# The last output projection of a decode kernel: two column strips, B's sum ahead of it, and five weight loads

## The chip, the cores and the metric

The kernel runs on one core of a Trainium2 chip (trn2). The time is what the device takes for one execution, in microseconds (us); executions of one kernel are repeated and the median is quoted. A profiled execution also gives a trace: what each engine did, when each DMA landed, and which share of its full clock TensorE was granted. "Span" is the time from the first to the last instruction in the trace; it is about 2 us shorter than the time.

PE is TensorE's matmul side, PEld its weight loads, DVE is VectorE, ACT ScalarE, SP SyncE (here the engine that issues the DMAs; SPq is its queue).

## The reference, cut to what matters

Two attention blocks decode one token each. Block A has 32 heads with 32768 keys; block B has 8 key/value heads for 32 query heads, with the last 4096 keys. Each ends in an output projection of a vector of 4096 values with a 4096x512 matrix, and the two results of 512 values are concatenated:

```python
def _A_ref(x, k_cache, v_cache, wq, wo):
    ...
    p = _softmax(scores, axis=-1)
    o = jnp.einsum("bhqk,bhkd->bhqd", p, v_cache)
    return (lambda x, *d: x.transpose(*d))(o, 0, 2, 1, 3).reshape(B, Sq, H * Dh) @ wo
# _B_ref: the same over the last W = 4096 keys, each key/value head used by four query heads
a = _A_ref(A_x, A_k_cache, A_v_cache, A_wq, A_wo)
b = _B_ref(B_x, B_k_cache, B_v_cache, B_wq, B_wo)
return jnp.concatenate([a, b], axis=-1)          # shape (1, 1, 1024), bf16
```

Caches and weights are bf16; what the kernel reads of them is 570 MB.

## The kernel before

The kernel streams K and V of A's 32 heads through on-chip buffers (8 MB each of K and V a head, back to back on SP's queue) and works on each head while the next arrives. B is done at the start, except for its output projection. After the last V the queue brings the two output matrices: B's in two loads, A's in four. Each output matrix lies as 128 partitions by 32 "rows" of 512 columns, so a projection is 32 matmuls that add up, each with one column of the attention vector as the 128x1 stationary operand and 512 weight columns as the moving operand. (This text calls one of those 32 steps a row.)

B's 32 rows run in four column strips of the array at once (output partitions 0, 32, 64, 96), whose four partial sums must be added at the end by one more matmul, with a column of ones and zeros (the trace shows it as two). A's 32 rows run one after the other, full width, into output partition 0.

```python
WO_CUTS = {"A": (0, 12, 22, 28, 32), "B": (0, 16, 32)}     # rows per load

def proj_part(self, name, part, out):
    a0, a1 = self.WO_CUTS[name][part:part + 2]
    ...
        for a in range(a0, a1):
            row, pos, begin, end = out(a)
            inst = e.matmul(row, lhsT=oz[:, a:a + 1], rhs=wo[:, 512 * a:512 * a + 512], start=begin, stop=end,
                            tile_position=pos, skip_group_check=True)
    return self.op("pe", mm, (self.wosem[name][part], 16), self.c[name]["ozop"])   # waits for that load

def store(self, name, bank, off, dep):
    o = self.op("dve", lambda v: v.tensor_copy(self.out_sb[0:1, off:off + 512], bank[0:1, :]), dep)
    self.op("sp", lambda e: e.dma_start(self.out[0, :, off:off + 512], self.out_sb[0:1, off:off + 512]) ..., o)

def emit_proj(self):
    for part in range(len(self.WO_CUTS["B"]) - 1):           # B: four strips
        o = self.proj_part("B", part, lambda a: (self.S[32 * (a % 4):32 * (a % 4) + 1, :], (0, 32 * (a % 4)), a < 4, a >= 28))
    strips = self.op("dve", lambda v: v.tensor_copy(self.pb[:, :], self.S[:, :]), o)
    for part in range(len(self.WO_CUTS["A"]) - 1):           # A: one full-width row after the other
        last = self.proj_part("A", part, lambda a: (self.PT[0:1, :], None, a == 0, a == 31))
        if part == 0:                                        # the sum of B's strips, after A's first part
            o = self.op("pe", lambda e: e.matmul(self.ACC[0:1, :], lhsT=self.e32[:, 0:1], rhs=self.pb[:, :], ...), strips, self.accread)
            self.store("B", self.ACC, 512, o)
    self.store("A", self.PT, 0, last)
```

## Time and profile before

| | before |
|---|---|
| median time, us | 1331.5 (six executions, 1329.72 to 1331.80) |
| span of the profiled execution (a seventh, 1331.99 us), us | 1329.9 |
| PE busy / DVE busy | 73% / 57% |
| DMA | busy almost throughout, 429 GB/s on average |
| A's last weights landed, us from the start | 1324.1 |
| A's last matmul done | 1327.6 |

The page's first two parts for the kernel before: the busy time of the engines, and the busy tenths of the DMA engines in 40 equal slices of the span.

```profile
PE 970.0 (73%) x13402; PEld 682.1 (51%) x13402; DVE 751.7 (57%) x1345; ACT 54.8 (4%) x167; POOL 2.3 (0%) x17
...
DMA  9999999999999999999999999999999999999997
```

The stream of bytes bounds the kernel: DMA is at 9 tenths or more in every slice but the last. Only in that last slice is there anything to gain in the projection, so all other views are of the last 14 us.

The DMA issues of the kernel before, over the end of the run: source and destination, count, size, and us from issue to landing.

```profile
kbuf<-in_A_wo_dram SPq DMA_DIRECT2D x1, 1536.0 KB, 28.1
kbuf<-in_A_wo_dram SPq DMA_DIRECT2D x1, 1280.0 KB, 30.8
kbuf<-in_A_wo_dram SPq DMA_DIRECT2D x1, 768.0 KB, 32.1
kbuf<-in_A_wo_dram SPq DMA_DIRECT2D x1, 512.0 KB, 32.9
```

They are issued at 1289.88, 1290.25, 1290.72 and 1291.21 us and land at 1317.93, 1321.03, 1322.85 and 1324.09.

The chain of waits that ended last, in order of time (start, length, what), of the kernel before:

```profile
1289.88 28.05 DMA kbuf<-in_A_wo_dram
1317.93 0.04 issue
1317.98 4.41 PE psPT L649 x12
1322.39 0.89 PE psACC L667 x2
1323.27 4.33 PE psPT L649 x20
1327.60 0.02 issue
1327.63 0.68 DVE out_sb L655
```

From the first landing on, PE never waits again: 12 rows, the sum of B's strips, 20 rows. It is 3.5 us (1327.60 - 1324.09) behind the last landing. Twelve rows took 4.41 us, but the last twenty 4.33 us; the windows say why. They give for each stretch its length, the busy time of PE, PEld, DVE, ACT and POOL (with counts), then the granted clock, the DMA share and GB/s.

```profile
1318.00:1321.00 3.00, 3.00 (x10) 1.01 (x11) 0.00 (x0) 0.00 (x0) 0.00 (x0) 0.65 0.91 370
1321.00:1322.00 1.00, 1.00 (x4) 0.28 (x3) 0.00 (x0) 0.00 (x0) 0.00 (x0) 0.50 0.45 186
1322.00:1323.00 1.00, 1.00 (x3) 0.21 (x2) 0.00 (x0) 0.00 (x0) 0.00 (x0) 0.84 0.25 100
```

PE got half its clock for about 3.4 us, from 1318.9 to 1322.3. A row of 512 columns takes 0.427 us there and 0.216 us at full clock, while a row's weights arrive every 0.31 us (20 rows in 6.1 us). So PE keeps up with the loads at full clock, and falls behind at half.

The end of the kernel before, from the timeline (start, length, engine, line, operation, tiles, count, and the idle time before it with what ended it):

```profile
1327.63 0.68 DVE L655 CAST out_sb<-psPT 1x512 bf16<-1x512 f32 x1 [3.64 <-PE psPT L649]
1328.33 0.25 SPq L656 DMA_DIRECT2D out_dram<-out_sb  x1
```

The store is issued at 1328.33 and, by the trace's completion records, lands at 1329.43, 1.10 us later.

### The profile page before, as it was taken

The page shows a single profiled execution, that of the slowest core. Times are in us where ns is not written, and L with a number is a line of the kernel's source. Part 1 is how long each engine was busy: PE and PEld are TensorE (multiplying, and loading weights), DVE is VectorE, ACT ScalarE, POOL GpSimd, SP SyncE. Part 2 cuts the span into 40 slices and gives each one's busy share as a digit, 9 for nine tenths or more (in the row PEclk, how much of TensorE's full clock was granted, in tenths as well). Part 3 has the DMA queues.
Part 4 walks back from the last instruction along what each step waited for, and adds up shares of the span by engine and source line. Part 5 has one row for each costly group of instructions (what it writes and reads, how often), then busy time and mean ns, then how long its engine had stood idle before and what let it go on. Part 6 is the DMA issues. An engine that isn't in the chain of part 4 may idle for free.

```text
span 1329.9 us, 28729 instructions
## 1 busy us (share of the span) xinstructions
PE 970.0 (73%) x13402; PEld 682.1 (51%) x13402; DVE 751.7 (57%) x1345; ACT 54.8 (4%) x167; POOL 2.3 (0%) x17
## 2 busy tenths in 40 slices
PE   3756678687677878767787876778777776877786
PEld 3544456554445655444465544446554444655552
DVE  3654466655556666554566655456665545666562
ACT  0000000000000000000000000000000000000000
POOL 0000000000000000000000000000000000000000
PEclk9767898878879887887988788798878779888888
DMA  9999999999999999999999999999999999999997
GB/s 391 432 432 435 437 428 432 436 438 430 432 434 434 436 432 434 430 440 432 434 430 440 432 432 430 442 430 434 430 440 432 432 432 440 432 432 432 433 435 306
DMA packets 12931, 570.66 MB, mean 429 GB/s; under 512 B 1522, under 2 KB 1524, under 8 KB 1780
## 3 DMA queue, kind: packets, MB, share of 16 engines
q1 hardware_dynamic: 12628, 570.43, 99.3%
q8 instruction: 12, 0.20, 0.1%
q10 hardware_dynamic: 288, 0.00, 0.0%
q14 instruction: 3, 0.02, 0.0%
HBM read 570.43 MB, written 0.00 MB: 429 GB/s over the span
## 4 chain that ended last, share of the span: by engine, by line
DMA 69%; PE 28%; DVE 2%; issue 0%; ACT 0%; SPq 0%
DMA kbuf<-in_A_k_cache_dram 64%; PE psT L491 24%; PE psS L513 4%; DMA kbuf<-in_B_k_cache_dram 3%; DMA kbuf<-in_A_wo_dram 2%; DVE kt L494 1%; PE psPT L649 1%; PE psACC L593 0%; SPq L286 0%; DVE oc_A L609 0%; PE psACC L667 0%; PE psPT L565 0%; ACT psb L541 0%; DVE tr_in L530 0%; DVE out_sb L655 0%
## 5 line engine op out<-in xcount | busy, mean ns | idle before, releaser
L494 DVE COPY kt<-psT 128x1024 bf16<-128x1024 bf16 x1056 | 656.5, 685 | 245.4 <-PE psT L491 243.8
L491 PE MATMUL psT<-ident,kbuf 128*128 128x128 bf16 x8448 | 582.9, 235 | 174.1 <-DMA kbuf<-in_A_k_cache_dram 162.1
L491 PEld LDWEIGHTS psT<-ident,kbuf 128*128 128x128 bf16 x8448 | 543.5, 107 | 266.5 <-DMA kbuf<-in_A_k_cache_dram 170.2
L593 PE MATMUL psACC<-vbuf,ptsb 128*4 128x512 bf16 (+1 forms) x2112 | 181.0, 517 | 22.8 <-ACT ptsb L568 22.0
L513 PE MATMUL psS<-kt,qw 128*32 128x512 bf16 x2048 | 157.6, 385 | 15.5 <-DVE kt L494 15.5
L607 DVE TENSOR_SCALAR oc_A<-psACC,hot_A 128x128 f32<-128x128 f32 x32 | 11.2, 351 | 245.0 <-PE psG L620 245.0
L593 PEld LDWEIGHTS psACC<-vbuf,ptsb 128*4 128x4 bf16 (+1 forms) x2112 | 58.6, 109 | 135.3 <-issue 84.9
L541 ACT ACTIVATE psb<-psS,nb_A 128x512 bf16<-128x512 f32 x32 | 22.0, 687 | 1170.0 <-DVE nb_A L540 1170.0
L513 PEld LDWEIGHTS psS<-kt,qw 128*32 128x32 bf16 x2048 | 34.0, 95 | 58.0 <-DVE kt L494 31.4
L620 PE MATMUL psG<-oc_A,hw 128*32 128x128 f32 (+1 forms) x128 | 19.3, 227 | 52.3 <-DVE oc_A L609 52.3
L620 PEld LDWEIGHTS psG<-oc_A,hw 128*32 128x32 f32 x128 | 11.4, 109 | 62.5 <-DVE oc_A L609 55.0
L565 PE MATMUL psPT<-ident,psb 128*128 128x128 bf16 x136 | 17.4, 268 | 34.0 <-ACT psb L541 34.0
L609 DVE SCALAR_TENSOR_TENSOR oc_A<-psACC,hot_A,oc_A 128x128 f32<-128x128 f32 x96 | 33.7, 351 | 3.4
L530 DVE TENSOR_REDUCE tr_in<-psS 128x1 f32<-128x512 f32 x34 | 23.5, 692 | 17.6 <-PE psS L513 17.6
L565 PEld LDWEIGHTS psPT<-ident,psb 128*128 128x128 bf16 x136 | 9.8, 114 | 37.1 <-ACT psb L541 36.7
L534 PE MATMUL psACC<-rows,tr_in 128*1 128x64 f32 x64 | 8.7, 217 | 25.5 <-DVE tr_in L530 25.5
L568 ACT ACTIVATE ptsb<-psPT 128x512 bf16<-128x512 bf16 x34 | 20.3, 597 | 28.9 <-PE psPT L565 28.9
L534 PEld LDWEIGHTS psACC<-rows,tr_in 128*1 128x1 f32 x64 | 2.7, 81 | 35.1 <-DVE tr_in L530 35.1
L538 PE MATMUL psACC<-mr_A,nscale 1*128 1x1 f32 x64 | 12.1, 256 | 9.7 <-DVE mr_A L537 9.7
L538 PEld LDWEIGHTS psACC<-mr_A,nscale 1*128 1x128 f32 x64 | 9.4, 182 | 15.7 <-DVE mr_A L537 15.7
L540 DVE COPY nb_A<-psACC 128x1 f32<-128x1 f32 x32 | 5.1, 158 | 15.0 <-PE psACC L538 15.0
L447 PE MATMUL psACC<-x_B,vbuf 128*128 128x1 bf16 x128 | 3.6, 165 | 13.6 <-DMA x_B<-in_B_x_dram 13.6
(71 smaller groups left out, 83.8 us busy)
## 6 DMA issues: line engine op xcount, KB each, us to landing
kbuf<-in_B_k_cache_dram SPq DMA_DIRECT2D x2, 4096.0 KB, 32.8
vbuf<-in_B_v_cache_dram SPq DMA_DIRECT2D x2, 4096.0 KB, 24.1
kbuf<-in_A_k_cache_dram SPq DMA_DIRECT2D x2, 4096.0 KB, 22.7
vbuf<-in_B_wq_dram SPq DMA_DIRECT2D x1, 4096.0 KB, 12.5
vbuf<-in_A_wq_dram SPq DMA_DIRECT2D x1, 4096.0 KB, 32.7
kbuf<-in_B_wo_dram SPq DMA_DIRECT2D x2, 2048.0 KB, 32.3
kbuf<-in_A_wo_dram SPq DMA_DIRECT2D x1, 1536.0 KB, 28.1
kbuf<-in_A_wo_dram SPq DMA_DIRECT2D x1, 1280.0 KB, 30.8
```

The source lines that it names most:

```text
L491: inst = e.transpose(T[:, 128 * k:128 * k + 128], src[:, DH * k:DH * k + DH], self.ident[:, :])
L494: self.copies.append(self.op("dve", lambda v: v.tensor_copy(KT[:, :], T[:, :]), o, to="pe"))
L513: inst = e.matmul(self.S[32 * c:32 * c + 32, :], lhsT=win, rhs=self.kt[(bb + c // 2) % NKT][:, 512 * (c % 2):512 * (c % 2) + 512], start=b ...
L530: o = dve(lambda v: v.reduce_max(tr["in"][:, 0:1], self.S[:, :], axis=AXX), self.sdone, self.k_pool, to="pe" if name == "A" else None)
L538: o = self.op("pe", lambda e: e.matmul(self.ACC[:, 64:65], lhsT=self.nscale[:, :], rhs=t["mr"][0:1, :], start=True, stop=True, skip_group_ ...
L541: self.sread = self.op("act", lambda s: s.activation(out=self.psb[:, :], in_=self.S[:, :], func=ACTF.Exp, bias=t["nb"][:, k:k + 1], scale= ...
L565: inst = e.transpose(PT[:, 128 * jj:128 * jj + 128], self.psb[:, 128 * jj:128 * jj + 128], self.ident[:, :])
L568: self.ptread = self.op("act", lambda s: s.activation(out=self.ptsb[:, :], in_=PT[:, 0:512], func=ACTF.Copy), self.psread, to="pe")
L593: inst = e.matmul(acc[32 * c:32 * c + rows, 0:512], lhsT=lhsT, rhs=rhs, start=begin, stop=end, tile_position=(0, 32 * c), skip_group_check ...
L609: o = self.op("dve", lambda v, src=src, hot=hot: v.scalar_tensor_tensor(out=oc, in0=src, scalar=hot, in1=oc, op0=ALU.mult, op1=ALU.add), p ...
L620: return self.op("pe", lambda e: e.matmul(self.G[0:32, c0 + c:c0 + c2], lhsT=win, rhs=t["oc"][g % 2][:, c:c2], start=False, stop=True, ski ...
L649: inst = e.matmul(row, lhsT=oz[:, a:a + 1], rhs=wo[:, 512 * a:512 * a + 512], start=begin, stop=end, tile_position=pos, skip_group_check=True)
```

## The change

The intent is to have almost nothing left to do when the last weights land. Each row of A becomes two matmuls of 256 columns in two column strips (output partitions 0 and 64) that can run side by side; the sum of B's strips goes ahead of A's projection; A's weights come in five loads with only three rows in the last one. The result now lies in two partitions, so VectorE copies 65x256, and the store moves two rows of 512 bytes in place of one of 1024.

```diff
-        self.out_sb = sb("out_sb", [1, 1024], BF16)
+        self.out_sb = sb("out_sb", [128, 512], BF16)
-    WO_CUTS = {"A": (0, 12, 22, 28, 32), "B": (0, 16, 32)}
+    WO_CUTS = {"A": (0, 11, 19, 25, 29, 32), "B": (0, 16, 32)}
 ...
+    def halves(self, e, bank, lhsT, rhs, begin, end):
+        for i in range(2):
+            inst = e.matmul(bank[64 * i:64 * i + 1, 0:256], lhsT=lhsT, rhs=rhs[:, 256 * i:256 * i + 256], start=begin,
+                            stop=end, tile_position=(0, 64 * i), skip_group_check=True)
+        return inst
     def store(self, name, bank, off, dep):
-        o = self.op("dve", lambda v: v.tensor_copy(self.out_sb[0:1, off:off + 512], bank[0:1, :]), dep)
-        self.op("sp", lambda e: e.dma_start(self.out[0, :, off:off + 512], self.out_sb[0:1, off:off + 512])
-                .then_inc(self.outsem[name], 16), o)
+        c = slice(off // 2, off // 2 + 256)
+        o = self.op("dve", lambda v: v.tensor_copy(self.out_sb[0:65, c], bank[0:65, 0:256]), dep)
+        self.op("sp", lambda e: e.dma_start(self.out[0, :, off:off + 512].rearrange("a (i x) -> (a i) x", i=2),
+                                            self.out_sb[0:65:64, c]).then_inc(self.outsem[name], 16), o)
 ... proj_part now calls out(e, weight column, weight row, a), which issues the matmuls; B's rows are as before
 ... emit_proj, after B's parts and the copy of its strips:
+        o = self.op("pe", lambda e: self.halves(e, self.ACC, self.e32[:, 0:1], self.pb, True, True), strips, self.accread)
+        self.store("B", self.ACC, 512, o)
         for part in range(len(self.WO_CUTS["A"]) - 1):
-            last = self.proj_part("A", part, lambda a: (self.PT[0:1, :], None, a == 0, a == 31))
-            if part == 0:
-                ...   # the sum of B's strips and its store
-        self.store("A", self.PT, 0, last)
+            o = self.proj_part("A", part, lambda e, lhsT, rhs, a: self.halves(e, self.PT, lhsT, rhs, a == 0, a == 31))
+        self.store("A", self.PT, 0, o)
```

More of the change, by code (lines that the diff above doesn't have):

```diff
@@ L647, in mm @@
             for a in range(a0, a1):
-                row, pos, begin, end = out(a)
-                inst = e.matmul(row, lhsT=oz[:, a:a + 1], rhs=wo[:, 512 * a:512 * a + 512], start=begin, stop=end,
-                                tile_position=pos, skip_group_check=True)
+                inst = out(e, oz[:, a:a + 1], wo[:, 512 * a:512 * a + 512], a)
             return inst
         return self.op("pe", mm, (self.wosem[name][part], 16), self.c[name]["ozop"])
+    def halves(self, e, bank, lhsT, rhs, begin, end):
[3 more added lines that the diff above has]
+        return inst
@@ L659, in emit_proj @@
     def emit_proj(self):
         for part in range(len(self.WO_CUTS["B"]) - 1):
-            o = self.proj_part("B", part, lambda a: (self.S[32 * (a % 4):32 * (a % 4) + 1, :], (0, 32 * (a % 4)), a < 4, a >= 28))
+            o = self.proj_part("B", part, lambda e, lhsT, rhs, a: e.matmul(
+                self.S[32 * (a % 4):32 * (a % 4) + 1, :], lhsT=lhsT, rhs=rhs, start=(a < 4), stop=(a >= 28),
+                tile_position=(0, 32 * (a % 4)), skip_group_check=True))
         strips = self.op("dve", lambda v: v.tensor_copy(self.pb[:, :], self.S[:, :]), o)
+        o = self.op("pe", lambda e: self.halves(e, self.ACC, self.e32[:, 0:1], self.pb, True, True), strips, self.accread)
@@ L664, in emit_proj @@
+        self.store("B", self.ACC, 512, o)
         for part in range(len(self.WO_CUTS["A"]) - 1):
-            last = self.proj_part("A", part, lambda a: (self.PT[0:1, :], None, a == 0, a == 31))
-            if part == 0:
-                o = self.op("pe", lambda e: e.matmul(self.ACC[0:1, :], lhsT=self.e32[:, 0:1], rhs=self.pb[:, :],
-                                                     start=True, stop=True, skip_group_check=True), strips, self.accread)
-                self.store("B", self.ACC, 512, o)
```

## The prediction

> **What bounds the kernel.** The stream of caches and weights: in the page's slices the DMA engines are 90% or more busy almost to the end, 570 MB in 1329.9 us, while PE is busy 73% and VectorE 57%. The change touches only the last 14 us, where the stream runs dry and TensorE finishes alone.
>
> **The tail before.** The timeline shows the four loads of A's output weights issued at 1289.88, 1290.33, 1290.72 and about 1291.2 us; the DMA issues give 28.1, 30.8, 32.1 and 32.9 us to landing, so they land at about 1318.0, 1321.1, 1322.8 and 1324.1. The chain of waits after the first landing is all PE: 12 rows 4.41 us (from 1317.98), the sum of B's strips 0.89, 20 rows 4.33 (to 1327.60), then a VectorE copy of 1x512, 0.68, then the store. PE ends 3.5 us after the last byte landed, because (windows) the granted clock is 0.50 from 1318.9 to 1322.3, where a 512-column matmul takes 0.427 us, against 0.216 afterwards. A row arrives every 0.31 us (6.1 us for 20 rows), so at half clock PE falls behind. The half clock follows PE's 2.65 us wait for the first load. The Trainium skill ("TensorE: Matmul & The Clock Gate", Part 1) says the clock halves after an idle window of about 3.4 us; the trace agrees in size.
>
> **What changes.**
> - Two strips of 256 columns should run side by side: per row about 0.11 us at full clock, 0.21 at half. The same page (Part 3) says column strips run concurrently; here four do: the PV product at half clock starts four matmuls per 0.427 us. Then even at half clock PE beats the loads (0.21 against 0.31 us) and the clock stops mattering. The 32 extra weight loads (31 to 50 ns each) hide.
> - The sum of B's strips leaves the chain: VectorE's copy of them ends at 1316.07, so the sum (about 0.45 us) ends by about 1316.7, before A's first load lands (11 rows, about 1317.7).
> - Five loads land at about 1317.7, 1320.2, 1322.0, 1323.3, 1324.1. After the last only 3 rows remain: 0.35 to 0.65 us. The fifth issue costs 0.44 us on the queue, far ahead of need. Bytes and the last landing stay.
> - The copy of 65x256 instead of 1x512: 0.68 to about 0.41 us. The store costs the same.
>
> **Sum.** PE ends at about 1324.1 + 0.05 + 0.65 = 1324.8 instead of 1327.6: 2.8 us. The copy gives 0.27. Together 3.1 us, all on the critical path, but 0.23% of the time. Predicted 1328.4 us, 8 in 10 between 1326.9 and 1330.0. Faster by over 2%: 0.01; within 2%: 0.98; slower: 0.01.
>
> **What would show it.** In the chain of waits the 9.6 us of PE become a DMA wait to about 1324, then under 1 us of PE. In the timeline the projection comes in five bursts, each after idle time ended by a DMA; B's sum stands before the first; the last copy takes about 0.4 us. If a row takes 0.43 us in a half-clock window, the strips don't overlap.
>
> **What would make it wrong.** The strips serialise, or weight loads between them stall PE: then little is gained beyond the removed sum. The last landing moves later, as smaller pieces (3 KB a partition) or the early store of B's half share the queue. The clock gate's phase differs from run to run: where before has no slow window there, it loses less and the gain shrinks. Run-to-run scatter (1329.7 to 1331.7) is as large as the gain.

## The result, and the profile after

The changed kernel took 1328.57 us (median of six executions, 1328.35 to 1329.03) against 1331.5 us (1329.72 to 1331.80) for the kernel before: 2.9 us less, against a predicted 3.1. The ratio is 0.9982, with a 95% interval of 0.9969 to 0.9995: the same within 2%, as predicted. A ratio here is the mean time of one kernel's fast runs over that of the other's of the same rounds, so it is not quite the ratio of the quoted medians: by the means of the six executions each the gain is 2.4 us, because two of the six before were of a faster level (below).

The chain of waits of the changed kernel:

```profile
1290.58 33.23 DMA kbuf<-in_A_wo_dram
1323.81 0.04 issue
1323.85 0.51 PE psPT L655 x6
1324.37 0.02 issue
1324.39 0.42 DVE out_sb L661
```

The 9.6 us of PE are gone from the chain. It now waits for the fifth load, and after that only 0.51 us of PE remain (six matmuls, three rows).

PE in the timeline of the changed kernel, from the sum of B's strips (psACC) on:

```profile
1317.68 0.60 PE L655 MATMUL psACC<-pb,e 128*1 128x256 f32 x4 [0.80 <-DVE pb L671]
1318.11 1.37 PE L655 MATMUL psPT<-kbuf,oz_A 128*1 128x256 bf16 x22
1319.83 1.04 PE L655 MATMUL psPT<-kbuf,oz_A 128*1 128x256 bf16 x16 [0.35 <-DMA kbuf<-in_A_wo_dram]
1321.70 0.82 PE L655 MATMUL psPT<-kbuf,oz_A 128*1 128x256 bf16 x12 [0.83 <-DMA kbuf<-in_A_wo_dram]
1322.91 0.60 PE L655 MATMUL psPT<-kbuf,oz_A 128*1 128x256 bf16 x8 [0.39 <-DMA kbuf<-in_A_wo_dram]
1323.85 0.49 PE L655 MATMUL psPT<-kbuf,oz_A 128*1 128x256 bf16 x6 [0.34 <-DMA kbuf<-in_A_wo_dram]
```

The projection comes in five bursts, four of them after idle time that a load ended. In the first burst 22 matmuls start within 1.10 us, so a row takes 0.11 us in place of 0.216: the strips do overlap. The Trainium skill ("TensorE: Matmul & The Clock Gate", Part 3) says that column strips run concurrently; this trace agrees, the two halves of a row starting 3 to 8 ns apart.

The windows of the changed kernel:

```profile
1318.00:1321.00 3.00, 2.52 (x42) 1.52 (x36) 0.42 (x1) 0.00 (x0) 0.00 (x0) 1.00 0.91 367
1321.00:1322.00 1.00, 0.30 (x6) 0.26 (x8) 0.00 (x0) 0.00 (x0) 0.00 (x0) 1.00 0.44 176
```

In this execution the clock happened to be 1.00 over the whole projection, so this pair of profiles alone can't say whether the strips or the clock made the difference. From 1318 on PE is no longer busy throughout: it waits for loads.

The DMA issues of the changed kernel, the first and the last of the five:

```profile
kbuf<-in_A_wo_dram SPq DMA_DIRECT2D x1, 1408.0 KB, 28.5
...
kbuf<-in_A_wo_dram SPq DMA_DIRECT2D x1, 384.0 KB, 33.2
```

The fifth, of 384 KB, is issued at 1290.58 and lands at 1323.81. The end of the changed kernel, from the timeline:

```profile
1324.39 0.42 DVE L661 CAST out_sb<-psPT 65x256 bf16<-65x256 f32 x1 [5.65 <-PE psPT L655]
1324.84 0.49 SPq L662 DMA_DIRECT2D out_dram<-out_sb  x1
```

The copy is shorter (0.42 us in place of 0.68), but the store takes longer: 0.49 us on the queue in place of 0.25, and it lands at 1326.34, 1.50 us after its issue in place of 1.10.

The difference of the two spans (1329.89 - 1326.81 = 3.08 us) adds up like this:

| term | before | after | gain, us |
|---|---|---|---|
| last landing | 1324.09 | 1323.81 | 0.28 |
| PE from there to its end | 3.51 | 0.55 | 2.96 |
| PE's end to the issue of the store (the copy) | 0.73 | 0.48 | 0.25 |
| issue of the store to its landing | 1.10 | 1.50 | -0.40 |
| landing to the end of the span | 0.46 | 0.47 | -0.01 |

The first term is scatter of the stream and not the change: B's last weights, which come before A's, had already landed 0.34 us earlier in this execution (1313.90 against 1314.24). Without it the spans would differ by 2.8 us, close to the 2.9 us of the medians.

### The profile page after: what moved, and what is told of

Same layout as the page of the kernel before. It is cut to its first block, busy times and chain, and to the rows that moved or that the text cites. A ratio compares the mean times of both kernels' runs of the same rounds, so it can differ in the third digit from the quotient of the medians.

```text
span 1326.8 us, 28797 instructions
## 1 busy us (share of the span) xinstructions
PE 964.5 (73%) x13436; PEld 679.5 (51%) x13436; DVE 749.8 (57%) x1345; ACT 54.8 (4%) x167; POOL 2.3 (0%) x17
## 4 chain that ended last, share of the span: by engine, by line
DMA 70%; PE 28%; DVE 1%; issue 0%; SPq 0%; ACT 0%
DMA kbuf<-in_A_k_cache_dram 65%; PE psT L491 23%; PE psS L513 4%; DMA kbuf<-in_B_k_cache_dram 3%; DMA kbuf<-in_A_wo_dram 3%; DVE kt L494 1%; PE psACC L593 0%; SPq L286 0%; DVE oc_A L609 0%; ACT psb L541 0%; DVE tr_in L530 0%; PE psPT L565 0%; ACT ptsb L568 0%; PE psPT L655 0%; PE psG L620 0%
## 5 line engine op out<-in xcount | busy, mean ns | idle before, releaser
L537 DVE TENSOR_REDUCE mr_A<-psACC 1x1 f32<-1x64 f32 x32 | 6.8, 213 | 11.7 <-PE psACC L534 11.7
```

## The experiments

Two things were open: which of the change's parts carries the 3 us, and why the kernel before has two levels of time (in its first six executions 1329.7 to 1330.0 and 1331.5 to 1331.8, nothing between). The theory of the prediction: half-clock stretches make full-width rows slower than their loads, and the strips make the end indifferent to the clock. The rivals: the reordering (B's sum out of the way, a small last load) does it, or the two together keep the clock up. Every kernel computes the right result except where it says so. The first and the third set share most of their executions of the kernel before.

### Two strips alone

The changed kernel with the old four loads and B's sum back after A's first part:

```diff
-    WO_CUTS = {"A": (0, 11, 19, 25, 29, 32), "B": (0, 16, 32)}
+    WO_CUTS = {"A": (0, 12, 22, 28, 32), "B": (0, 16, 32)}
 # emit_proj: the sum of B's strips stands after A's part 0 again (as halves)
```

> Two half-width strips alone, with the old four loads and B's sum still after A's first part. Theory (the strips' speed is the gain: a row costs 0.11 us at full and 0.21 us at half clock, both under the 0.31 us in which it arrives): PE ends about 0.7 us after the last landing whatever the clock, the time is within 0.3 us of the changed kernel's, 1328.4 to 1328.9 us. Rival (moving B's sum and the five loads carry the gain): 1330 us or more, and PE busy without a break after the first landing.

Measured: 1329.08 us (1328.91 to 1329.42, four executions), ratio 0.9982. The profile fell on a half-clock stretch in the middle of the projection. A window of it:

```profile
1318.00:1321.00 3.00, 3.00 (x28) 1.58 (x28) 0.00 (x0) 0.00 (x0) 0.00 (x0) 0.56 0.91 367
```

The first and the last burst of PE in its timeline:

```profile
1317.95 2.72 PE L655 MATMUL psPT<-kbuf,oz_A 128*1 128x256 bf16 x24 [1.81 <-DMA kbuf<-in_A_wo_dram]
...
1324.11 0.60 PE L655 MATMUL psPT<-kbuf,oz_A 128*1 128x256 bf16 x8 [0.42 <-DMA kbuf<-in_A_wo_dram]
```

At half clock the 24 matmuls start within 2.30 us, twelve rows with 11 steps between them, so 0.21 us a row, less than the 0.31 us in which a row arrives. PE caught up and waited again before the last two loads; it ended 0.66 us after the last landing (1324.07). The mechanism is as predicted, though the median lies 0.2 us above the expected range.

### B's sum ahead and five loads, without strips

```diff
-    WO_CUTS = {"A": (0, 12, 22, 28, 32), "B": (0, 16, 32)}
+    WO_CUTS = {"A": (0, 11, 19, 25, 29, 32), "B": (0, 16, 32)}
 # emit_proj: the full-width sum of B's strips and its store stand before the loop over A's parts
```

> The other two parts alone: B's sum ahead, five loads, one full-width matmul a row. Theory: PE still needs 0.427 us a row in a half-clock window and falls behind the loads there; it ends 1 to 3 us after the last landing; time 1329.3 to 1331, depending on where the half-clock window falls. Rival (these two parts carry the gain): PE ends under 1 us after the last landing, time about 1328.6 us.

Measured: 1329.14 us (1328.93 to 1329.17, four executions), ratio 0.9982. That is the rival's level, and the equal of the strips alone. In its profile the clock was 1.00 over the projection, and PE still ended 0.87 us after the last landing, with no wait between the rows. Four times that close together could be a clock kept up by the sum, or luck; so it was run again, with its own expectation:

> The run with B's sum ahead and five loads once more, for more times: its four lay between 1328.93 and 1329.17. Theory B (the sum keeps the clock up): again within 0.4 us of each other, near 1329.1. Rival (those four had luck with the clock's phase): some times over 1329.8.

Measured: 1328.86, 1330.39, 1330.14, 1329.79 and 1330.70 us. The first four had been luck: without strips the same kernel spreads over 1.8 us. Only the first of these was profiled (clock 1.00 over the projection, PE's end again 0.87 us after the last landing), so the slower ones are put down to the clock by the theory, not by a trace of theirs. Its ratio in this set is 0.9998, where the same kernel had 0.9982 before, partly because six of this set's nine executions of the kernel before were of its faster level. A ratio of such mixtures says little at this size; ranges and traces say more.

### Each of the two alone

Five loads alone change one line (the cuts, as above). B's sum ahead alone moves the sum, with the four loads.

> The kernel before with the five loads and nothing else (full-width matmuls, B's sum still after A's first part). PE works without a break from the first landing, which comes 0.3 us earlier with 11 rows in place of 12. Theory: the cuts alone are worth that 0.3 us, as PE is behind the loads anyway; most runs near 1331.2, PE ending over 3 us after the last landing in a half-clock run. Rival (the small last load is what helps): 1329.3 us or less.

Measured: 1331.04 us (1329.40 to 1331.42, four executions), ratio 1.0000. The profile has a half-clock stretch from about 1313.4 to 1320.2, and PE ends 2.9 us after the last landing. The half-clock profile misses the expected "over 3 us" by little. The ratio shows no gain from the cuts alone, but it mixes two levels of time. Level by level the four lie a little lower: 1331.02, 1331.07 and 1331.42 where the slower level of the kernel before in this set is 1331.49 to 1331.83, and 1329.40 under its faster one, 1329.67 to 1330.19. So the cuts may well be worth the expected 0.3 us; four executions don't settle it.

> The kernel before with B's sum moved ahead of A's first part and nothing else. Theory A: the sum is 0.86 us of PE work that leaves the stretch after the first landing, and no more: times in two groups as before, each 0.9 us earlier, 1328.9 and 1330.6. Theory B: the sum, standing in PE's wait of 2.65 us for the first load, also keeps the half clock away from A's projection: one group only, about 1329.3 us, with the clock at 1.0 over all of A's projection in the profile.

Measured: 1329.43, 1330.05, 1331.16 and 1329.70 us (median 1329.88), ratio 0.9998. Neither theory fits as written. There is no single group, so the sum doesn't keep the clock up reliably (theory B falls). Nor are these the two groups of theory A: one time lies above both. The trace shows why the sum's 0.86 us can't be had in every execution; its chain of waits:

```profile
1313.43 3.20 PE psS L649 x32
...
1317.40 1.02 PE psACC L664 x2
1318.42 7.01 PE psPT L649 x32
```

Here the half clock fell on B's rows (psS), which took 3.20 us in place of about 2. The sum, which must follow them, then stood in front of A's first part, whose weights had landed at 1317.80. PE works in order: what goes ahead can also block. The changed kernel's own profile has the same thing (its sum delays A's first part to 1318.11, with the weights there at 1317.29), but with strips PE catches up within that first burst.

### No sum at all

Five loads and full-width rows, with B's sum and the copy before it left out, so B's half of the result is wrong. This keeps the wait before A's first load long while no sum stands on either side of it.

> Wrong on purpose: five loads, full-width matmuls, B's sum left out altogether (B's output is its first strip alone), so that PE's wait before A's first load is as long as before (about 2.3 us) but no sum follows the first landing. Theory A (only the sum's work counts): one level with the run that has the sum ahead and five loads, about 1329.1 us in all runs. Theory B (the sum keeps the clock up): some runs have a half-clock window on A's projection and end 1 to 2 us later, near 1330.5, with PE ending over 2 us after the last landing.

Measured: 1330.11, 1330.54, 1329.11, 1330.43 and 1330.49 us (median 1330.43). In its timeline, the wait for A's first load and the start of the burst:

```profile
1317.22 3.22 PE L649 MATMUL psPT<-kbuf,oz_A 128*1 128x512 bf16 x10 [2.35 <-DMA kbuf<-in_A_wo_dram]
```

And its windows:

```profile
1315.08:1318.49 3.41, 1.27 (x6) 0.51 (x7) 0.53 (x1) 0.00 (x0) 0.00 (x0) 1.00 1.00 411
1318.49:1321.90 3.41, 3.41 (x9) 1.02 (x8) 0.00 (x0) 0.00 (x0) 0.00 (x0) 0.50 0.76 305
```

After a wait of 2.35 us the half clock came 1.3 us into the burst (at about 1318.5), and the 32 rows took 8.77 us in place of 6.9 (32 times 0.216). PE ended 2.2 us after the last landing, with no sum involved. So the sum's work is not what makes PE late; the half clock on full-width rows suffices. That fits the second half of theory B's expectation. Whether the sum in the gap makes such stretches rarer stays open: the kernel with the sum and five loads had five times from 1328.86 to 1329.17 out of nine, this one had one of five under 1329.2, too few to say (the clock records, below, say more).

### Keeping PE busy

The kernel before, with ten idle full-width matmuls into an unused bank while PE waits for A's first load:

```diff
+        def warm(e):
+            for a in range(10):
+                inst = e.matmul(self.T[1][0:1, :], lhsT=self.c["B"]["oz"][:, a:a + 1],
+                                rhs=self.kbuf[:, 512 * a:512 * a + 512], start=True, stop=True, skip_group_check=True)
+            return inst
+        self.op("pe", warm, (self.wosem["B"][0], 16), self.c["B"]["ozop"], self.copies[-1])
```

> The kernel before with ten idle full-width matmuls into an unused bank, to keep PE busy while it waits for A's first load (about 2.2 us at full clock). Theory (the half clock makes PE fall behind): the clock over A's projection is 1.0, a row costs 0.216 us, PE ends 1.0 to 1.6 us after the last landing in place of 3.5, time about 1329.3 us. Rival (the order of the work and the width of the last part, not the clock): PE still ends about 3.5 us after the last landing, time as before, 1331.5 us.

Measured: 1329.56, 1330.94, 1331.78 and 1331.30 us (median 1331.12), ratio 0.9999. As a remedy it fails, in three executions of four. The profiled one is the first, 1329.56 us, with the clock at 1.00 over the projection. Its chain of waits is the kernel before at full clock:

```profile
1317.62 2.75 PE psPT L649 x12
1320.38 0.86 PE psACC L673 x2
1321.23 4.33 PE psPT L649 x20
1325.57 0.02 issue
```

The same work that took 9.62 us in the profile of the kernel before takes 7.95 us, and PE ends 1.83 us after the last landing (1323.74) in place of 3.5, a little over the expected 1.0 to 1.6. The execution lasted 1329.56 us, the level of the kernel before's faster group. The three slow executions have no trace; ten matmuls at half clock would take 4.3 us (ten times 0.427) and delay A's first part themselves, but that is argued and not shown.

### The kernel before, twice more

> The kernel before once more, for a second profile. Its six times fall into two groups, 1329.7 to 1330.0 and 1331.5 to 1331.8 us. Theory: they differ by whether a half-clock window of about 3.4 us falls on A's projection; this profile has either such a window and a time near 1331.6, with PE ending about 3.5 us after the last landing, or none and a time near 1329.8, with about 1.7 us. Rival: the two groups differ in the stream (the last landing is later), and PE's distance to it is 3.5 us in both.

> The kernel before once more: both profiles of it so far were of the slower group (span 1329.7 and 1329.9, half clock from about 1318.5 to 1322). Theory (the groups are the clock's phase): if this one is of the faster group (span about 1328.0), the clock is 1.0 over A's projection and PE ends 1.6 to 2.0 us after the last landing; if it is of the slower group, as before. Rival (something else makes the groups): a faster one with a half-clock window in the same place, or with an earlier last landing.

Measured: 1331.38 and 1331.56 us (single executions, so of unknown state), spans 1329.7 and 1329.7, both of the slower level. Both show half clock for about 3.4 us from about 1318.1 and 1317.9 on, and PE ending 3.5 us after the last landing. So three of three slow executions with a trace have the half-clock stretch on the projection. No fast one of the unchanged kernel came before the profiler; the nearest is the run above with idle matmuls. The arithmetic fits: at full clock 32 rows at 0.216 us and the sum's 0.86 us take 7.8 us in place of 9.6, and the groups lie 1.7 us apart. In all sets no time of the kernel before lies between 1330.2 and 1331.3 us; one, 1332.79, lies 0.8 us above the rest of the slower level and has no trace.

The clock records of the kept traces say what such a stretch follows. In all 14 traces every complete record lasts a whole multiple of 3.41 us (1838 records), so the clock changes only on a grid of 3.41 us, and this grid lies differently against the kernel in each execution. Two neighbouring stretches of the grid in the kernel before:

```profile
1315.50:1318.91 3.41, 0.93 (x5) 0.41 (x6) 0.57 (x1) 0.00 (x0) 0.00 (x0) 1.00 1.00 417
1318.91:1322.32 3.41, 3.41 (x10) 1.04 (x9) 0.00 (x0) 0.00 (x0) 0.00 (x0) 0.50 0.70 286
```

The stretch with the idle matmuls in the run above:

```profile
1315.53:1318.94 3.41, 2.90 (x15) 0.95 (x14) 0.19 (x1) 0.00 (x0) 0.00 (x0) 1.00 1.00 413
```

PE was busy for 27% of the first, and half clock followed; it was busy for 85% of the last, and full clock followed. Counted over all full-clock stretches of the grid in the 14 traces: after those with PE busy for less than 44%, half clock followed in 775 of 775; after those with more than 52%, in none of 2487; in between it is mixed. (Busy time is as the profile models it. This is a count over traces that were there; no run was made to test it.) So in these traces what counts is PE's busy share in one stretch of the grid, and a wait that the grid happens to cut in two can pass without half clock: the wait around 1311 us was followed by half clock in the changed kernel (a stretch at 37%), but in the run with the sum and five loads the grid divided it between stretches at 50% and 63%, and the clock stayed full. It also bears on the sum in the gap: in the two profiles with the sum ahead and five loads no 3.41 us that end between 1316 and 1324 us have PE busy for under 60%, where the kernel before has as little as 22%. An estimate from that: with B's rows at full clock, a half-clock stretch couldn't begin on A's projection there. It could still begin on B's rows, as in the profile of the sum alone; the slow executions of that kernel have no trace.

### The changed kernel again, and with a one-row store

The variant gives the halves back to one row on the way out: VectorE copies the first half and ScalarE at the same time the second, from partition 64 to partition 0, and one row of 1024 bytes is stored. PE's last matmul of the second strip signals ScalarE, the one before it VectorE.

```diff
+        o = self.op("dve", lambda v: v.tensor_copy(self.out_sb[0:1, off:off + 256], bank[0:1, 0:256]), first)
+        p = self.op("act", lambda s: s.activation(
+            out=self.out_sb[0:1, off + 256:off + 512], in_=bank[64:65, 0:256], func=ACTF.Copy), second)
+        self.op("sp", lambda e: e.dma_start(self.out[0, :, off:off + 512], self.out_sb[0:1, off:off + 512])
+                .then_inc(self.outsem[name], 16), o, p)
```

> The changed kernel again, to be compared with its variant on the same chip. Theory (strips make the end indifferent to the clock's phase): all times within 0.8 us, 1328.3 to 1329.1, PE ending 0.5 to 0.7 us after the last landing wherever the half-clock window lies. Rival: with more times a second group appears, 1 us or more above.

> The changed kernel with its two halves copied into one row, the first by VectorE and the second by ScalarE at the same time, and stored as one row of 1024 bytes. In the traces so far the last store takes 1.10 us from issue to landing as one row (queue 0.25 us) and 1.50 as two rows of 512 bytes (queue 0.49). Theory (two rows cost 0.4 us): landing 1.1 us after the issue, the time 0.3 to 0.4 us under the changed kernel's of this job, about 1328.2 us. Rival (the length of the store doesn't end the span, or ScalarE's copy gives it back): no difference over 0.1 us.

Measured in the same set: the changed kernel 1328.97 us (1328.79 to 1329.55, five executions), the variant 1328.61 us (1328.13 to 1328.79, six executions), the kernel before 1331.67 us (seven executions). Ratios to before: 0.9982 and 0.9979. The variant is 0.36 us faster by the medians, and the two ranges only touch. A window of the variant:

```profile
1318.00:1321.00 3.00, 3.00 (x36) 1.69 (x30) 0.07 (x1) 0.07 (x1) 0.00 (x0) 0.55 0.90 361
```

Its end, from the timeline:

```profile
1324.38 0.41 DVE L657 CAST out_sb<-psPT 1x256 bf16<-1x256 f32 x1 [6.31 <-PE psPT L653]
...
1324.86 0.25 SPq L660 DMA_DIRECT2D out_dram<-out_sb  x1
```

The store lands at 1325.97, 1.11 us after its issue, against 1.50 us in the changed kernel's new profile. So two rows cost 0.4 us, and this can be had back. The extra time lies early: the first completion record comes 0.41 us after the issue of the one-row store and 0.91 after that of the two-row store, the last one 0.70 and 0.59 us later. The Trainium skill ("DMA: Bandwidth & Descriptors", the section on why a DMA increments its semaphore by 16) says that the number of DMA engines follows from the slowest dimension of the transfer, and that the rest of the sixteen counts is written at once. The traces agree: the one-row store has two completion records, the two-row store three.

The same profiles settle the clock. In the variant the clock was about half from 1313.9 to 1320.7, over the first two loads' rows; in the new profile of the changed kernel it was 1.00 throughout. PE ended 0.55 us after the last landing in both (1323.81 to 1324.36, 1323.93 to 1324.49). Of eleven times of the changed kernel one, 1329.55, lies 0.5 us above the next; a second group 1 us up has not appeared.

### A guess at the last landing

In every trace of the two kernels, three or four of the sixteen partial completions of each of A's weight loads come 1.1 to 1.5 us after the rest (three in the first load, mostly four in the others; the expectation below says three). The idea was to take bytes away from the late DMA engines, by splitting the last two loads by partitions:

```diff
-        self.load(self.kbuf[:, ...], src[:, ...], ...)
+        for p0, p1 in ((0, 108), (108, 128)) if name == "A" and part >= 3 else ((0, 128),):
+            self.load(self.kbuf[p0:p1, ...], src[p0:p1, ...], ...)
```

> On top of the one-row store: the last two loads (7 rows) are split by partitions into 108 and 20. In every trace three of a load's sixteen partial completions come 1.2 to 1.5 us after the other thirteen. A guess: the split takes bytes from the three DMA engines that are late. If so, the last landing comes up to 0.8 us earlier and the time falls to about 1327.5 us; if the late three are among those that get more, it comes up to 1 us later. No other theory is tested.

Measured: 1331.71 us (1331.30 to 1331.84), 3.1 us slower than without the split. The last load landed at 1326.45, 2.5 us later than in the changed kernel of the same set, more than the expected 1 us. Even the load ahead of the split ones, itself unsplit, landed at 1323.55 against 1321.78. The guess was wrong. The two pieces of a split load left 24 completion records where a whole load leaves 16, so the split also changed on how many DMA engines the last rows ran. That may be why they came later; it was not tested. Which engines are late, and why, is open.

## Why the prediction was right

The time came out at 1328.57 us for a predicted 1328.4, and the gain at 2.9 us for 3.1. Point by point:

- **The tail bounds the gain.** "PE ends 3.5 us after the last byte landed" before, and 0.7 us was predicted for after. Measured: 3.51 and 0.55 us. This is 2.96 of the 3.08 us between the two spans.
- **The strips overlap.** Predicted 0.11 us a row at full and 0.21 at half clock; measured 0.11 and 0.21, so the 32 extra weight loads hid as well.
- **The clock stops mattering.** Right in the traces: the strips alone and the one-row variant had half clock on the projection and still ended 0.66 and 0.55 us after the last landing. Without strips, the work of the kernel before ended 1.83 us after the last landing at full clock (the run with idle matmuls) and 3.5 us after it with a half-clock stretch.
- **The half clock follows PE's wait.** It was there after the waits of 2.65 us (before) and 2.35 us (no sum). Both are shorter than the 3.4 us that the prediction names; it is the half-clock stretch that lasts 3.41 us. And putting work into the wait didn't give the faster level reliably. By the clock records what counts is PE's busy share in the stretch of the 3.41 us grid before: 27% and 37% in these two. What places the grid is open.
- **The sum leaves the chain.** In the profile it is 0.89 us of PE's 9.6, and it did leave. Its place was mis-timed: predicted to end by 1316.7, it ended at 1318.11, 0.8 us after A's first weights landed, because B's rows were at half clock. With strips this cost nothing.
- **The five loads.** The last landing stayed, as predicted: measured from the landing of B's weights it came 9.91 us later in place of 9.85. Alone they gave nothing that the ratio shows (perhaps a few tenths of a us, level by level); with the strips, the last load leaves three rows (0.51 us of PE) where four loads leave four (0.62 us).
- **The copy.** Predicted 0.68 to 0.41 us; measured 0.68 to 0.42.
- **"The store costs the same."** This step failed: two rows cost 0.40 us more than one (1.50 against 1.10). The sum came out right by luck: PE ended 0.15 us sooner after the last landing than assumed and the last landing came 0.28 us earlier, by the scatter of the stream, in the profiled execution; the medians, with 2.9 us for the predicted 3.1, show the rest of it.
- **The scatter.** The prediction named the clock's phase as what could shrink the gain. It does: against the slower level of the kernel before (about 1331.6) the gain is 3 us, against its faster level (about 1329.9) 1.3 us. The change also narrows the time, from a spread of 2.1 us in the first six executions to 0.7 us (1.2 us over all eleven). So the size of the gain depends on how the levels happen to mix: 2.9 us by the medians, 2.4 by the means.

## What to carry to other kernels

At the end of a stream, count what an engine still has to do after the last byte lands, and compare its time per piece with the time in which a piece arrives, at the worst clock that the traces show. If it is faster than the arrival even then, the end no longer depends on the clock; reordering around a slower step helps in some executions only. In these traces the clock went by PE's busy share in each 3.41 us, so a gap is best judged by that share and not by its length alone. And look at the form in which the result leaves: splitting it over two partitions saved 0.26 us in the copy and gave 0.40 us back in the store.

## What the Trainium skill lacked or had wrong

- "TensorE: Matmul & The Clock Gate" (Part 1, and the table near its end) ties the fall to half clock to an idle window of about 3.4 us, and advises against idle gaps over about 3 us. Here gaps of 2.35 and 2.65 us were followed by half clock, 1.3 and 0.9 us after the work had begun again; PE had been busy for 37% and 27% of the 3.41 us before, not idle. The stretches' length of 3.4 us agrees (1318.9 to 1322.3).
- "DMA: Bandwidth & Descriptors" tells how many engines a transfer of few rows uses, but not what a second row costs in latency: a 1 KB store took 1.10 us from issue to landing as one row and 1.50 as two, and its issue 0.25 and 0.49 us.
- "DMA: Bandwidth & Descriptors" (latency and other measured facts) names two engines that are usually slower, with a best guess at the cause that only the software-driven path has. Here, on a hardware queue (q1 hardware_dynamic in the pages), three or four of the sixteen completions of each of A's weight loads came 1.1 to 1.5 us after the rest, in all traces of the two kernels; splitting the last loads by 108 and 20 partitions made the last landing 2.5 us later.
- "TensorE: Matmul & The Clock Gate" (Part 3) has measured speedups for three column strips and for more tiles, none for two column strips; for two strips of 256 columns the runs show 0.11 us a row in place of 0.216 at full clock, and 0.21 in place of 0.427 at half.
